# Delta-rule attention into a SwiGLU block on one core: products, sums and bank clears put in another order

## The chip, the cores and the metric

The kernel runs on one core of a Trainium2 chip. Its engines work side by side, each through its own queue in order: TensorE (PE in the profile; PEld is its weight loads), VectorE (DVE), ScalarE (ACT), GpSimd (POOL) and SyncE (SP), which issues the DMAs. The metric is the time of one execution on the device in microseconds (us); less is better. Before the change three executions took 687.78 us in the median (686.82 to 689.39).

## What is computed

Everything is float32. A delta-rule attention over 4 batches, 8 heads, 768 steps and a head size of 48 gives 3072 tokens of 384 numbers, and these go through a SwiGLU block with a hidden size of 1536:

```python
for t in range(S):
    kt, vt, bt = (k_n[:, :, t], v[:, :, t], beta[:, :, t, None])
    y[:, :, t] = np.einsum('bhd,bhde->bhe', q[:, :, t], state)
    v_old = np.einsum('bhde,bhd->bhe', state, kt)
    state = state + bt[:, :, :, None] * np.einsum('bhd,bhe->bhde', kt, vt - v_old)
...
g = x @ w_gate
silu = g * (1.0 / (1.0 + np.exp(-g)))
val = x @ w_val
return (silu * val @ w_out).astype(np.float32)
```

## The kernel before

**Tiling.** The 768 steps are cut into 12 chunks of 64 steps. A chunk has 4 x 64 = 256 tokens, which the kernel treats as two blocks of 128. The order of instructions on every engine is written out by hand: the order of the Python calls is the order in each engine's queue, and an instruction waits in its queue for the results it needs.

**What runs in a chunk.** For chunk c the feed-forward block runs: gate and value products, the elementwise product h, and the output product. Between its parts the attention of chunk c + 1 is slipped in by `point(c + 1)`, one step at a time: a step of `advance` (four in all; the last one transposes the result on TensorE and ScalarE copies it to `x_ffn`, the input x of the next chunk's feed-forward block, L1152 and L1153), or a step of preparation (transposes of keys and queries on VectorE, L470, and their products on TensorE, L497; a join, L870 to L888). `fill(n)` adds steps of a triangular inverse, with transposes on VectorE (L551) and a long run of small operations on GpSimd (L580, L586). Some points have a step left for TensorE and some have none.

**Rounds.** From chunk 2 on the gate and value products use a fast matrix product that needs fewer multiplications. `gate_val_fast(c, r, fill)` is one such round and makes six of the 24 blocks of h. Chunk 2 has one round (r = 0), the chunks 3 to 11 have two (r = 0 and r = 1): 19 rounds in all. A round is a fixed sequence of 15 products, named by number here as in the code: `multiply(p, n, c, r)` is product n, accumulated into the PSUM bank p. It is four matmuls, which the profile lists as eight matmul instructions of L1280 with eight weight loads. The banks are p4 (later called p2), p3 (later p6), p0 and p1 (later p5). Between the products VectorE adds and subtracts in PSUM (`plus` is L1510, `minus` is L1507) and ScalarE copies banks to the temporaries t0 and t1. `finish_h` lets ScalarE take the silu of one half of a bank (L1316) and VectorE multiply it with the other half (L1317). In a round the order on TensorE is: 4, 13, 1, 3, 2, a point, then 7, 11, 9, 0, 5, a point, then 6, 10, 8, 14, a point; product 12 follows at the head of the next round or of the output.

The banks tie products to VectorE. Product 5 accumulates into p0, where product 11 has put its result, so it can't start before `minus(t1, t1, p0)` has read p0. Product 6 accumulates into p0 again and can't start before `minus(p5, t0, p0)` has read what product 5 left. Product 8 goes into p6, which is the bank p3 where product 0 ended: `finish_h(c, r, 5, p3)` must have read it, and `minus(p6, t0, p2)` must have filled it anew.

**Sums of x.** Products 4, 3, 9, 14, 7, 5, 10, 6 and 8 take sums of blocks of x as their moving operand. `sums_of_x(c)` makes ten of them on VectorE; the first four (for products 3, 9, 14 and 4) are a chain, each adding to the one before. `x_sums(c)` calls it once, at the first call at which the four steps of `advance` for that chunk have been issued. `begin(c)` starts a chunk with product 4, which needs the fourth sum of the chain, then product 13, which needs none.

**Output.** `output_fast(c, fill)` has seven products of 12 matmuls with 192 columns (L1557). Two of its banks, p[1, 0] and p[1, 1], are begun by ScalarE writing zeros (`clear`, L1549), since the products that go in only accumulate. For the chunks after 2 the order is: first product, product 3, 2, 4, 5, a point, 6, the addition of the left half of o[1], its store, `x_sums(c + 1)`, product 7. In chunk 2 it is: first product, 5, 4, a point, 2, 3, a point, 7, store, `x_sums(3)`, 6, store. `first_product` clears p[1, 0], issues the product, copies it out and clears p[1, 1].

## Time and profile before

| what | value |
|---|---|
| median of three executions | 687.78 us (686.82 to 689.39) |
| the profiled execution | 689.76 us |
| its span, first to last instruction | 688.1 us |
| mean granted TensorE clock | 0.992 |
| DVE busy | 473.3 us (69%) |
| ACT busy | 256.1 us (37%) |
| POOL busy | 201.7 us (29%) |
| matmuls of L1280 on x_t and w_gv | 760, 102.4 us busy |
| matmuls of L1557 on wo_sb and h_f | 480, 84.2 us busy |
| sums and differences of 128x512 in PSUM, L1507 (ffn from p_sb and ffn) | 36, median 692 ns |
| sums of x, 128x128 (x_t from x_t and x_ffn, L1510) | 30, median 293 ns |

The profile shows one execution. Its own time, 689.76 us, is 1.7 us above its span, and 2.0 us above the median of the three. Matmuls overlap, so an instruction of 275 ns starts every 112 ns: the time of a product is read from one product's start to the next one's (0.89 us), not from the sum of its instructions. In rows of the timeline the first two numbers are start and duration in microseconds, then engine, line and operation, the tiles written and read, and in brackets how long the engine had been idle before and what ended that.

| stretch, us | PE busy | DVE busy | ACT busy | POOL busy | PE clock |
|---|---|---|---|---|---|
| 0 to 170 | 155.21 | 119.87 | 94.03 | 40.59 | 0.98 |
| 170 to 224 (chunk 2) | 50.74 | 40.52 | 17.86 | 38.56 | 0.97 |
| 280 to 330 (chunk 4) | 48.04 | 35.29 | 18.45 | 29.11 | 1.00 |
| 330 to 384 (chunk 5) | 53.21 | 35.12 | 16.88 | 11.81 | 1.00 |
| 540 to 590 (chunk 9) | 50.00 | 27.68 | 15.41 | 0.00 | 1.00 |

### The profile page before, as it was taken

How to read it: one execution, taken by the hardware profiler on the slowest of the kernel's cores; microseconds unless marked ns; L12 is line 12 of the kernel's file. 1: busy time of each engine (PE TensorE's matmuls, PEld its weight loads, DVE VectorE, ACT ScalarE, POOL GpSimd, SP SyncE). 2: the span in 40 equal slices, each digit the busy share in tenths (PEclk: the TensorE clock that was granted, in tenths of full speed). 3: DMA queues.
4: the chain of work that ended last, by engine and by line, in shares of the span. 5: the costliest groups of instructions: out<-in, count | busy, mean ns of one | idle time of the engine just before them, and what ended most of it. 6: DMA issues, size and time to landing. Idle time of an engine off the chain costs nothing.

```text
span 688.1 us, 24813 instructions
## 1 busy us (share of the span) xinstructions
PE 653.7 (95%) x10850; PEld 603.7 (88%) x10850; DVE 473.3 (69%) x982; ACT 256.1 (37%) x546; POOL 201.7 (29%) x309
## 2 busy tenths in 40 slices
PE   7788999998999999999999999999999999999997
PEld 4566888756988899999999999999999999999997
DVE  7987778798569867757767747767657655645462
ACT  5785765214332332334332244332232333132130
POOL 7130031104883030881030881030882000000000
PEclk9998999999999999999999999999999999999999
DMA  9767824016226352276262176242187122132220
GB/s 135 169 176 190 243 94 137 1 35 136 45 45 164 73 136 64 49 156 143 54 134 74 45 153 138 60 110 80 26 171 152 48 88 78 40 100 71 76 71 23
DMA packets 147437, 68.55 MB, mean 100 GB/s; under 512 B 123457, under 2 KB 126561, under 8 KB 147329
## 3 DMA queue, kind: packets, MB, share of 16 engines
q1 hardware_dynamic: 144992, 66.48, 40.2%
q8 instruction: 85, 1.39, 0.8%
q10 hardware_dynamic: 2080, 0.39, 0.4%
q0 software_dynamic: 256, 0.10, 0.1%
q14 instruction: 24, 0.19, 0.1%
HBM read 59.08 MB, written 7.86 MB: 97 GB/s over the span
## 4 chain that ended last, share of the span: by engine, by line
PE 64%; DVE 3%; issue 0%; DVEq 0%
PE ffn L1280 36%; PE ffn L1557 17%; PE p_px L1073 1%; PE p_px L1054 1%; PE p_py L497 1%; PE p_py L1127 1%; PE p_py L1044 1%; DVE x_t L1510 1%; DVE ffn L1507 1%; PE p_px L902 1%; PE p_px L497 1%; PE p_py L1152 1%; PE p_py L884 1%; PE p_px L870 1%; DVE o_sb L1510 0%
## 5 line engine op out<-in xcount | busy, mean ns | idle before, releaser
L1280 PE MATMUL ffn<-x_t,w_gv 128*128 128x128 f32 x760 | 102.4, 278 | 6.6 <-DVE x_t L1507 6.6
L1280 PEld LDWEIGHTS ffn<-x_t,w_gv 128*128 128x128 f32 x760 | 93.1, 193 | 8.3 <-issue 5.8
L1557 PE MATMUL ffn<-wo_sb,h_f 128*128 128x192 f32 x480 | 84.2, 329 | 0.6 <-ACT ffn L1549 0.6
L811 POOL TENSOR_TENSOR n_b<-mb,half 128x32 f32<-128x32 f32 x5 | 27.6, 5520 | 191.3 <-DVE mb L551 191.3
L1280 PE MATMUL ffn<-x_ffn,w_gv 128*128 128x128 f32 x600 | 80.0, 277 | 0.0
L1557 PEld LDWEIGHTS ffn<-wo_sb,h_f 128*128 128x128 f32 x480 | 77.8, 190 | 1.6 <-ACT ffn L1549 0.9
L1316 ACT ACTIVATE sil<-ffn 128x256 f32<-128x256 f32 x95 | 34.5, 382 | 114.6 <-PE ffn L1280 106.6
L586 POOL TENSOR_TENSOR zb<-zb,h_f 128x31 f32<-128x31 f32 (+15 forms) x124 | 71.9, 580 | 9.7
L1280 PEld LDWEIGHTS ffn<-x_ffn,w_gv 128*128 128x128 f32 x600 | 73.8, 194 | 0.0
L580 POOL TENSOR_TENSOR h_f<-zb,mb 128x31 f32<-128x31 f32 (+15 forms) x124 | 69.4, 560 | 14.4 <-DVE mb L568 5.0
L1280 PE MATMUL ffn<-x_t,h_f 128*128 128x128 f32 x464 | 63.6, 280 | 3.9 <-DVE ffn L1507 3.9
L1317 DVE TENSOR_TENSOR h_f<-sil,ffn 128x256 f32<-128x256 f32 x95 | 37.6, 418 | 42.8 <-ACT sil L1316 42.8
L1280 PEld LDWEIGHTS ffn<-x_t,h_f 128*128 128x128 f32 x464 | 56.3, 192 | 5.9 <-DVE ffn L1507 4.9
L1440 PE MATMUL ffn<-x_ffn,w_gv 128*128 128x256 f32 x216 | 48.0, 381 | 0.0
L1440 PEld LDWEIGHTS ffn<-x_ffn,w_gv 128*128 128x128 f32 x216 | 40.7, 190 | 5.6
L1510 DVE TENSOR_TENSOR o_sb<-o_sb,ffn 128x192 f32<-128x192 f32 x49 | 17.1, 349 | 31.5 <-PE ffn L1557 31.0
L1510 DVE TENSOR_TENSOR ffn<-ffn,p_sb 128x512 f32<-128x512 f32 x36 | 24.8, 693 | 16.2 <-PE ffn L1280 15.1
L1557 PE MATMUL ffn<-last_k,h_f 128*128 128x192 f32 x200 | 35.8, 326 | 0.0
L1440 PE MATMUL ffn<-x_t,w_gv 128*128 128x256 f32 x144 | 35.7, 400 | 0.0
L1557 PEld LDWEIGHTS ffn<-last_k,h_f 128*128 128x128 f32 x200 | 32.8, 190 | 0.0
L1440 PEld LDWEIGHTS ffn<-x_t,w_gv 128*128 128x128 f32 x144 | 27.7, 199 | 4.0
L1280 PE MATMUL ffn<-x_ffn,h_f 128*128 128x128 f32 x224 | 30.0, 277 | 0.0
(343 smaller groups left out, 1165.2 us busy)
## 6 DMA issues: line engine op xcount, KB each, us to landing
h_f<-w_s SPq DMA_DIRECT2D x81, 256.0 KB, 2.7
more_w<-w_s SPq DMA_DIRECT2D x27, 256.0 KB, 2.9
vin<-in_v_dram SPq DMA_DIRECT2D x48, 96.0 KB, 3.5
out_dram<-o_sb SPq DMA_DIRECT2D x48, 96.0 KB, 2.2
kn<-in_k_dram SPq DMA_DIRECT2D x20, 192.0 KB, 4.7
w_s<-h_f SPq DMA_DIRECT2D x10, 256.0 KB, 3.2
zt<-in_moe_w_out_dram SPq DMA_DIRECT2D x6, 384.0 KB, 4.4
qpad<-in_q_dram SPq DMA_DIRECT2D x36, 64.0 KB, 3.2
```

The lines of the kernel that those rows point to most:

```text
L497: nc.tensor.matmul(p_v[par][half_of(b if of_q else b ^ par), bp, j], kt[c][half_of(par), bp, j, b], xt[half_of(par), bp, j, b],)
L580: engine.tensor_tensor(out=t_v, in0=zb[:, 0 : j + 1, j : j + 1].to_broadcast([128, j + 1, m]), in1=mb[:, j : j + 1, j + 1 : R].to_broadcas ...
L586: engine.tensor_tensor(out=zb[:, 0 : j + 1, j + 1 : R], in0=zb[:, 0 : j + 1, j + 1 : R], in1=t_v, op=ALU.add,)
L811: nc.gpsimd.tensor_tensor(out=n, in0=mb.rearrange("p j i -> p (j i)")[:, 0 : R * R : R + 1], in1=half, op=ALU.pow,)
L870: nc.tensor.matmul(p_j[dst, c, m], a[lo, c, 2 * m + e, 0:R], zt[lo, c, 2 * m + e, R:C],)
L884: nc.tensor.matmul(p_j[hi, e, c, m], z1[row, c, m], t2[row, c, m])
L1280: nc.tensor.matmul(p[:, u], w(u), moving, start=start and u == 0, stop=True, skip_group_check=True,)
L1316: nc.scalar.activation(silu_of, p[:, 0:2], ACTF.Silu)
L1317: nc.vector.tensor_tensor(out=h_of(c, PAIRS[r][e % 3], e // 3), in0=silu_of, in1=p[:, 2:4], op=ALU.mult)
L1440: nc.tensor.matmul(ps[name][:, i], w_sb[:, t, (f + i) * 128 : (f + i + 1) * 128], xts[c][:, t], start=(t == 0 and i == 0), stop=(t == KT - 1),
L1510: nc.vector.tensor_tensor(out=out, in0=a, in1=b, op=ALU.add)
L1557: nc.tensor.matmul(p[x, part], a(f - f % 2)[:, f % 2], b(f), start=not begun and f == 0, stop=f == FH - 1, skip_group_check=True,)
```

## The change

Four things are put in another order; no operation is added or taken away.

1. In every round product 5 is issued ahead of product 0, and `minus(p5, t0, p0)` ahead of `finish_h(c, r, 5, p3)`. `load_late()`, which issues a waiting DMA if there is one, stays between the two products.
2. The chain of four sums of x is a function of its own. In the output of the chunks after 2 it is issued right behind product 6, ahead of the addition that empties p[1, 0]; the other six sums stay where all ten were.
3. In the output of chunk 2 all ten sums for chunk 3 are issued ahead of the second point and of product 7, instead of behind them.
4. In chunk 2 p[1, 1] is cleared together with p[1, 0], ahead of the first product, instead of behind the copy of that product's result.

```diff
-    def sums_of_x(c):
+    def first_sums_of_x(c):
         x = sums_x
         plus(x[3], x_of(c, 0, 0), x_of(c, 0, 2))
         plus(x[9], x[3], x_of(c, 1, 0))
         plus(x[14], x[9], x_of(c, 1, 2))
         minus(x[4], x[14], x_of(c, 1, 1))
+
+    def sums_of_x(c):
+        x = sums_x
         plus(x[8], x_of(c, 0, 0), x_of(c, 1, 0))
...
-    summed = set()
+    begun, summed = set(), set()
+
+    def first_x_sums(c):
+        if c < NCH and c not in begun and steps("advance", c) >= 4:
+            begun.add(c)
+            first_sums_of_x(c)
 
     def x_sums(c):
-        if c < NCH and c not in summed and steps("advance", c) >= 4:
+        first_x_sums(c)
+        if c in begun and c not in summed:
             summed.add(c)
             sums_of_x(c)
...
         multiply(p2, 9, c, r)
         minus(t1, t1, p0)
+        multiply(p0, 5, c, r)
+        load_late()
         multiply(p3, 0, c, r)
-        load_late()
-        multiply(p0, 5, c, r)
+        minus(p5, t0, p0)
         finish_h(c, r, 5, p3)
-        minus(p5, t0, p0)
         minus(p6, t0, p2)
...
         def first_product():
             clear(0)
+            if c == FAST:
+                clear(1)
             product(0, 0, lambda f: h_of(c, f, 0), quarter(0, 0))
             nc.scalar.copy(o[0][:, right], p[0, 0])
             more_sums_of_h(c)
             if c > FAST:
                 end_of_rounds()
-            clear(1)
+                clear(1)
...
             product_6()
+            first_x_sums(c + 1)
             plus(o[1][:, left], o[0][:, right], p[1, 0])
             store(c, 1, o[1])
             x_sums(c + 1)
...
             plus(o[1][:, right], o[1][:, right], p[1, 0])
+            x_sums(c + 1)
             point(c + 1)
             product_7()
             store(c, 0, o[0])
-            x_sums(c + 1)
             product_6()
```

## The prediction

> **What bounds the kernel now.** I read the page's busy times first, then who waited for whom on PE, then the chain that ended last, then the timeline at the places that these name.

> ```profile
> PE 653.7 (95%) x10850; PEld 603.7 (88%) x10850; DVE 473.3 (69%) x982; ACT 256.1 (37%) x546; POOL 201.7 (29%) x309
> ```
> ```profile
> PE ffn L1280 <- DVE ffn L1507: 7.9, 10, 0.8
> PE ffn L1280 <- DVE x_t L1507: 6.6, 5, 1.8
> ```

> PE is busy for 95% of the span: only its gaps can be won without removing work. From chunk 2 on, two waits (columns: us in total, times, longest) hold nearly all of them: ten in front of a product of L1280 for a subtraction in PSUM, and five for the last of the chained sums of x. The first kind in a round of chunk 4:

> ```profile
> 311.47 1.06 PE L1280 MATMUL ffn<-x_ffn,w_gv 128*128 128x128 f32 x8
> ...
> 312.36 1.06 PE L1280 MATMUL ffn<-x_t,h_f 128*128 128x128 f32 x8
> ...
> 312.56 0.69 DVE L1507 TENSOR_TENSOR p_sb<-p_sb,ffn 128x512 f32<-128x512 f32 x1 [1.31 <-PE ffn L1280]
> ...
> 313.14 0.97 PEld L1280 LDWEIGHTS ffn<-x_ffn,w_gv 128*128 128x128 f32 x8
> 313.25 1.06 PE L1280 MATMUL ffn<-x_ffn,w_gv 128*128 128x128 f32 x8
> ...
> 314.15 1.06 PE L1280 MATMUL ffn<-x_t,w_gv 128*128 128x128 f32 x8
> 314.35 0.38 ACT L1316 ACTIVATE sil<-ffn 128x256 f32<-128x256 f32 x1 [1.68 <-PE ffn L1280]
> ...
> 314.76 0.42 DVE L1317 TENSOR_TENSOR h_f<-sil,ffn 128x256 f32<-128x256 f32 x1 [1.51 <-ACT sil L1316]
> 315.24 1.29 DVE L1507 TENSOR_TENSOR ffn<-p_sb,ffn 128x512 f32<-128x512 f32 x2
> 315.99 0.97 PEld L1280 LDWEIGHTS ffn<-x_t,more_w 128*128 128x128 f32 x8 [0.98 <-DVE ffn L1507]
> 315.99 1.16 PE L1280 MATMUL ffn<-x_t,more_w 128*128 128x128 f32 x8 [0.79 <-DVE ffn L1507]
> ```

> The PE rows are products 11, 9, 0, 5 and 6. A product starts 0.89 us after the one before; its first weight load runs 0.11 ahead of it (313.14 to 313.25). Product 5 ends at 315.20, the subtraction into p5 starts at 315.24 and takes 0.69 (two share the row), and the load of product 6 comes 0.05 after its end. The load was due at 314.15 + 0.89 - 0.11 = 314.93 and came at 315.99: 1.06 us lost. Ten of the 19 rounds show this; in the other nine an attention step of PE lies between products 5 and 6.

> The second kind, at the end of chunk 3, and the clear in chunk 2:

> ```profile
> 281.63 2.11 PE L1557 MATMUL ffn<-wo_sb,h_f 128*128 128x192 f32 x12
> 281.83 0.35 DVE L1510 TENSOR_TENSOR o_sb<-o_sb,ffn 128x192 f32<-128x192 f32 x1 [1.38 <-PE ffn L1557]
> 282.10 0.72 DVE L1510 TENSOR_TENSOR x_t<-x_ffn 128x128 f32<-128x128 f32 x1
> ...
> 284.15 0.62 DVE L1507 TENSOR_TENSOR x_t<-x_t,x_ffn 128x128 f32<-128x128 f32 x1
> ...
> 284.88 0.97 PEld L1280 LDWEIGHTS ffn<-x_t,w_gv 128*128 128x128 f32 x8 [1.43 <-issue]
> ```
> ```profile
> 216.06 0.33 ACT L1549 COPY ffn<-mask_q 128x192 f32<-128x192 f32 x1
> ...
> 216.44 3.87 PEld L1557 LDWEIGHTS ffn<-wo_sb,h_f 128*128 128x128 f32 x24 [0.93 <-ACT ffn L1549]
> ```

> Product 7 of the output starts at 281.63, twelve matmuls at 0.1625 apart; the load of product 4 was due at 283.47 and came at 284.88, 0.11 after the fourth sum: 1.41 lost.

> **Part 1, products 5 and 0 exchanged.** Removed: 10 x 1.06 = 10.6 us, since product 0 (0.89) now lies between 5 and 6. Left of it: product 5's end to the load of product 6 still takes 0.04 + 0.69 + 0.05 = 0.78, while the load is due 0.89 - 0.11 - 0.16 = 0.62 after that end (a product ends 0.16 after the next one's start, 312.52 against 312.36). So 0.16 stays, ten times: 1.6 us.

> Added: product 5 must now follow `minus(t1, t1, p0)` behind product 9 alone. Before, 9 and 0 covered it. In the rows above the subtraction ends at 313.25, the load could come at 313.30 and is due at 313.14: 0.16 late. VectorE starts it 0.04 after product 11 in 16 of 19 rounds. In three (chunks 3, 5 and 7, r = 1) a copy of the join stands in front: it runs from 359.92 to 361.14, the subtraction to 361.86, the load comes at 361.91 instead of 361.44, 0.47 late. That makes 16 x 0.16 + 3 x 0.47 = 3.9 us. No row has a subtraction covered by just one product; from below the price is 0 (the load doesn't wait; a wait that is added can't gain), from above 1.06 per round (as where nothing covers it). I take the worked value: the same operation on the same bank type ends the ten waits.

> Queued behind the waits: product 0 waits with product 5, so the silu of `finish_h` starts 0.16 later than before and, on VectorE, behind the subtraction into p5. Does product 8 wait for it? In the round shown: load of 5 at 313.30, product 0 at 314.30, its end 315.36, silu 315.40 to 315.78, multiplication 315.81 to 316.23, subtraction into p6 to 316.85 at most. Product 6 comes at 315.25, 10 at 316.25, and the load of 8 is due at 317.03. That is 0.13 to spare; if it were gone, 0.1 to 0.3 in ten rounds. The VectorE work behind it ends 0.3 later while PE is 0.74 earlier. Where two transposes of L470 (2.4 us) follow, ScalarE's last silus and copies are that late too, and the clear of p[1, 0] behind them (323.61 to 323.92) moves to 324.03, for a load that was due at 324.62 and is now due at 323.88: 0.2 lost in chunks 4, 6 and 8, 0.6 us. `load_late` passes no reload (products 0 and 5 issue none), so SP's order stays.

> Part 1: 10.6 - 1.6 - 3.9 - 0.6 = 4.5 us gained.

> [...] The row at 315.99 shows the load waiting with its matmul, so I go by the row.

> **Part 2, chain of sums first.** Waits of this kind that the change can reach stand ahead of chunks 4, 6 and 8 (1.41 each) and of chunk 3; the fifth, ahead of chunk 2, is not touched. For chunks 5, 7, 9, 10 and 11 the sums are in time already (0.29 each, not 0.63). Behind the change the chain can start when x_ffn is copied (280.67 in chunk 3) and takes the 2.67 it took (282.10 to 284.77): done at 283.34, load 283.45, due 283.47. Gain 3 x 1.41 = 4.2 us at most, 0 at least: no sum comes later than it did. The addition behind the chain ends at 283.7 instead of 282.2; the copy that needs its bank comes after product 4 (ends 284.7). The store waits as long, and the reload queued behind it on SP is for a form used some ten products later.

> **Parts 3 and 4, chunk 2.** The load of output product 5 was due at 215.43 and came at 216.44; the second clear now runs behind the first, ended by 215.6, load at 215.65: 0.8 gained. Product 4 of chunk 3 was due at 228.90 and came at 230.30: 1.4. But the transposes of L470 now come behind ten sums, some 2.8 us later: keys are ready at 230.4 (229.7 with the 0.7 that chunk 2's round gains), and their product is due at 229.2. So 0.5 is given back: 1.7 together, from 0.3 to 2.2.

> **Sum.** 4.5 + 4.2 + 1.7 = 10.4 us. Against the profiled execution: span 688.1 to 677.7, time 689.76 to 679.4. The profiled execution lies 2.0 above the median; off the median it is 687.8 - 10.4 = 677.4.

> **Rivals.** (a) Only matmuls wait and loads run ahead of the wait: 29 waits are 0.11 shorter, 3.1 us, so 674.3. For it: at 284.88 the load came 0.03 ahead of its matmul (284.91). Against: in all ten waits for a PSUM bank the load came with the matmul. [...] (b) VectorE is late everywhere as in the three join rounds: 29 waits at 0.47 cost 13.6, part 1 becomes 10.6 - 13.6 - 0.6 = -3.6, and the whole gains 2.3: 685.5. For it: PE's gaps were VectorE's time to catch up, and the margins (0.13 at product 8, 0.02 at product 4) are thin. Against: in 16 rounds VectorE had been waiting for PE. (c) The chain isn't early, since `first_x_sums` does nothing unless the fourth step has been issued: 4.2 lost, 681.6. Against: the transposes of that step (L1152) stand ahead of product 6 in all these chunks. (d) Slower: product 5 becomes the wait of every round, VectorE still working off transposes and sums of h when product 11 ends. Each 0.1 us of lateness costs 2.9 us over the 29 waits, so it decides from 0.36 on; at 0.7 (half a transpose of L551, 1.2) it is 20.3 - 10.4 = 9.9 worse, 697.7. Against: in the busiest stretch with such rounds, 280 to 330, DVE is busy for 35.3 of 50 us.

> **How the numbers follow.** Forecast 0.58 (674.5 to 680.5 by itself), (a) 0.12, (b) 0.12, (c) 0.10, (d) 0.08. What a measurement can tell from no change is about 0.5%, 3.4 us: below 684.3 is faster, above 691.2 slower. Faster: forecast, (a), (c), 0.80; same: (b), 0.12; slower: (d), 0.08. The range leaves out (b) and (d), 0.20: from 673 (rival (a) and the 1 us by which runs differ) to 684.5.

> **What would show it.** No wait of 0.8 before product 6, but 19 short ones before product 5, product 9 to product 5 at 0.94 instead of 0.89, and 1.00 from there to product 0. The wait for x_t gone ahead of chunks 3, 4, 6 and 8. Wrong would be: a wait above 0.3 before product 5 or any before product 8; sums of x still behind the addition; the granted clock below 0.99.

## The result, and the profile after

The changed kernel takes 681.86 us in the median of five executions (679.86 to 684.13); the kernel before, run beside it, 687.78 (686.82 to 691.36). The ratio is 0.989, 95% interval 0.985 to 0.993: faster by 5.9 us, where 10.4 were forecast. The interval is a gain of 4.7 to 10.0 us, so the forecast gain lies just outside it.

The profiled executions have spans of 688.1 and 680.2 us, 7.9 apart. 2.06 of that lies ahead of 160 us, where the change touches nothing: the kernel before ran for 6.8 us at half TensorE clock there, from 62.9 on, the changed one for 3.4, from 37.5 on. From 160 us on the changed kernel is 5.84 ahead, and from here on only this is compared: the start of one and the same instruction in two traces, counted from an attention product (L1054) at about 160 us. The mean granted clock is 0.992 in both.

The busy times of the page after:

```profile
PE 657.2 (97%) x10850; PEld 606.2 (89%) x10850; DVE 474.5 (70%) x982; ACT 255.7 (38%) x546; POOL 197.1 (29%) x309
```

PE's share rose from 95 to 97%, but its busy time rose too, by 3.5 us, for the same instructions: what was won can't be read from this view.

The waits of weight loads after (us in total, times, longest):

```profile
PEld ffn L1290 <- DVE ffn L1520: 2.0, 1, 2.0
...
PEld ffn L1290 <- DVE ffn L1517: 1.6, 10, 0.2
...
PEld ffn L1290 <- DVE p_sb L1517: 1.2, 3, 0.4
```

Lines have moved by ten: L1290 is `multiply`, L1517 `minus`, L1520 `plus`. The ten waits of 0.8 have become ten of 0.16, as forecast; the three of 0.4 are the join rounds. The first line is new, and nothing forecast it. Of PE's five waits for sums of x, 6.6 us in all, one is left, ahead of chunk 2, which the change doesn't touch:

```profile
PE ffn L1290 <- DVE x_t L1517: 1.8, 1, 1.8
```

The round of chunk 4 that was shown of before, in the timeline of after:

```profile
309.95 1.06 PE L1290 MATMUL ffn<-x_t,h_f 128*128 128x128 f32 x8
...
310.90 1.16 PE L1290 MATMUL ffn<-x_t,w_gv 128*128 128x128 f32 x8
...
311.89 1.06 PE L1290 MATMUL ffn<-x_ffn,w_gv 128*128 128x128 f32 x8
...
312.16 0.70 DVE L1517 TENSOR_TENSOR ffn<-p_sb,ffn 128x512 f32<-128x512 f32 x1 [1.32 <-PE ffn L1290]
...
312.91 0.97 PEld L1290 LDWEIGHTS ffn<-x_t,more_w 128*128 128x128 f32 x8 [0.16 <-DVE ffn L1517]
312.92 1.16 PE L1290 MATMUL ffn<-x_t,more_w 128*128 128x128 f32 x8
```

These are products 9, 5, 0 and 6: 0.95 from 9 to 5 (forecast 0.94), 0.99 from 5 to 0 (1.00), and product 0 covers all but 0.16 of the subtraction into p5. The end of chunk 3, PE alone: product 4 of chunk 4 comes 1.95 after the output's product 7, twelve matmuls at 0.1625, without a wait.

```profile
280.48 2.11 PE L1567 MATMUL ffn<-wo_sb,h_f 128*128 128x192 f32 x12
282.43 1.05 PE L1290 MATMUL ffn<-x_t,w_gv 128*128 128x128 f32 x8
```

And the place that lost: products 2, 7, 11, 9 and 5 of chunk 3's round 0, PE alone, then the windows of the same time (PE, PEld, DVE, ACT and POOL busy, then the granted clock):

```profile
232.19 1.06 PE L1290 MATMUL ffn<-x_ffn,w_gv 128*128 128x128 f32 x8
235.06 1.77 PE L1290 MATMUL ffn<-x_t,h_f 128*128 128x128 f32 x8 [1.81 <-DVE ffn L1520]
236.63 1.91 PE L1290 MATMUL ffn<-x_ffn,w_gv 128*128 128x128 f32 x8
238.34 1.30 PE L1290 MATMUL ffn<-x_t,more_w 128*128 128x128 f32 x8
239.47 1.06 PE L1290 MATMUL ffn<-x_t,w_gv 128*128 128x128 f32 x8
```
```profile
235.00:236.00 1.00, 0.94 (x6) 0.94 (x7) 0.61 (x2) 0.63 (x2) 0.00 (x0) 0.71 0.87 158
236.00:237.00 1.00, 1.00 (x6) 1.00 (x6) 0.00 (x0) 0.13 (x1) 0.00 (x0) 0.50 0.98 109
```

PE waits 1.81 us for `plus(p1, p0, t0)`, and the three products behind it take 1.57, 1.71 and 1.13 instead of 0.89 to 0.95: the granted clock is 0.71 and 0.50 in the windows shown, and 0.50 in the next. The kernel before had neither the gap nor the half clock here (products 7, 11, 9 and 0 at 237.48, 238.48, 239.37 and 240.26).

Term by term, from 160 us on (minus is a gain):

| term | forecast, us | measured, us |
|---|---|---|
| ten stalled rounds | -7.4 (-0.74 each) | -6.7 (-0.63 in chunk 2, -0.67 in the others) |
| six rounds without a stall | +1.0 (+0.16 each) | +0.9 (+0.15 each) |
| three join rounds | +1.4 (+0.47 each) | +1.4 (+0.46 each) |
| clear of p[1, 0] in chunks 4, 6 and 8 | +0.6 (0.2 each) | +0.3 (0.14 in 4 and 6, none seen in 8) |
| sums ahead of chunks 4, 6 and 8 | -4.2 (-1.41 each) | -4.2 (-1.40 or -1.41 each) |
| parts 3 and 4 | -1.7 | +1.75 |
| PE idle at L870 in chunk 5, with `issue` alone named (last section) | none | +0.76 |
| sum | -10.4 | -5.8 |

Of the ten stalled rounds one, chunk 3's round 0, lies inside the stretch of parts 3 and 4. It is taken at -0.67, and the 1.75 is what is left. That stretch runs from the last L902 product ahead of chunk 2's output (211.79 in the trace before) to the first join product L870 of chunk 3 (246.77): 34.97 us before, 36.05 after, and 36.05 - 34.97 + 0.67 = 1.75.

### The profile page after: what moved, and what is told of

Read it like the earlier page. It is cut to its first block, busy times and chain, and to the rows that moved or that the text cites. A ratio compares the mean times of both kernels' runs of the same rounds, so it can differ in the third digit from the quotient of the medians.

```text
span 680.2 us, 24832 instructions
## 1 busy us (share of the span) xinstructions
PE 657.2 (97%) x10850; PEld 606.2 (89%) x10850; DVE 474.5 (70%) x982; ACT 255.7 (38%) x546; POOL 197.1 (29%) x309
## 3 DMA queue, kind: packets, MB, share of 16 engines
q8 instruction: 85, 1.39, 0.8%
## 4 chain that ended last, share of the span: by engine, by line
PE 90%; DVE 6%; ACT 2%; issue 2%; DVEq 0%
PE ffn L1290 38%; PE ffn L1567 20%; PE ffn L1450 11%; PE ffn L1477 4%; PE p_px L1054 2%; PE p_px L1073 2%; PE p_py L1044 1%; PE p_px L902 1%; PE p_py L497 1%; PE p_py L1127 1%; PE p_px L497 1%; PE p_py L1152 1%; PE p_px L631 1%; PE p_px L870 1%; PE p_py L884 1%
## 5 line engine op out<-in xcount | busy, mean ns | idle before, releaser
L1290 PE MATMUL ffn<-x_t,w_gv 128*128 128x128 f32 x760 | 103.5, 280 | 2.4 <-DVE x_t L1517 1.8
L1290 PEld LDWEIGHTS ffn<-x_t,w_gv 128*128 128x128 f32 x760 | 93.1, 192 | 4.7 <-DVE x_t L1517 2.0
L1290 PE MATMUL ffn<-x_ffn,w_gv 128*128 128x128 f32 x600 | 81.0, 279 | 0.0
L580 POOL TENSOR_TENSOR h_f<-zb,mb 128x31 f32<-128x31 f32 (+15 forms) x124 | 71.0, 572 | 14.4 <-DVE mb L568 5.0
L1290 PEld LDWEIGHTS ffn<-x_ffn,w_gv 128*128 128x128 f32 x600 | 74.7, 196 | 0.0
L586 POOL TENSOR_TENSOR zb<-zb,h_f 128x31 f32<-128x31 f32 (+15 forms) x124 | 69.5, 561 | 9.7
L1290 PE MATMUL ffn<-x_t,h_f 128*128 128x128 f32 x464 | 64.2, 282 | 1.8 <-DVE ffn L1520 1.8
L1290 PEld LDWEIGHTS ffn<-x_t,h_f 128*128 128x128 f32 x464 | 56.9, 193 | 3.7 <-DVE ffn L1520 2.0
L1517 DVE TENSOR_TENSOR ffn<-p_sb,ffn 128x512 f32<-128x512 f32 x36 | 25.1, 696 | 24.4 <-PE ffn L1290 23.8
L1520 DVE TENSOR_TENSOR ffn<-ffn,p_sb 128x512 f32<-128x512 f32 x36 | 24.7, 692 | 19.4 <-PE ffn L1290 16.2
L1450 PE MATMUL ffn<-x_t,w_gv 128*128 128x256 f32 x144 | 33.9, 385 | 0.0
L1520 DVE TENSOR_TENSOR o_sb<-o_sb,ffn 128x192 f32<-128x192 f32 x49 | 16.9, 347 | 20.6 <-PE ffn L1567 20.2
L1290 PE MATMUL ffn<-x_ffn,h_f 128*128 128x128 f32 x224 | 30.3, 279 | 0.0
```

What stands on the lines that cost most here:

```text
L580: engine.tensor_tensor(out=t_v, in0=zb[:, 0 : j + 1, j : j + 1].to_broadcast([128, j + 1, m]), in1=mb[:, j : j + 1, j + 1 : R].to_broadcas ...
L586: engine.tensor_tensor(out=zb[:, 0 : j + 1, j + 1 : R], in0=zb[:, 0 : j + 1, j + 1 : R], in1=t_v, op=ALU.add,)
L1290: nc.tensor.matmul(p[:, u], w(u), moving, start=start and u == 0, stop=True, skip_group_check=True,)
L1450: nc.tensor.matmul(ps[name][:, i], w_sb[:, t, (f + i) * 128 : (f + i + 1) * 128], xts[c][:, t], start=(t == 0 and i == 0), stop=(t == KT - 1),
L1517: nc.vector.tensor_tensor(out=out, in0=a, in1=b, op=ALU.subtract)
L1520: nc.vector.tensor_tensor(out=out, in0=a, in1=b, op=ALU.add)
```

## The experiments

Two theories of chunk 3's start stood against each other. T1: VectorE has no idle time left between chunk 2's rounds and `plus(p1, p0, t0)`, so whatever PE gains on the way comes back as a wait at product 7, and one long wait is followed by half clock. T2: the parts add up as forecast, and what is missing is chance. For T1 speak the windows of VectorE in the trace before (busy time, instructions, clock, DMA share, GB/s):

```profile
205.00:210.00 5.00, 4.90 (x8) 1.00 0.64 81
...
215.00:220.00 5.00, 4.93 (x8) 1.00 0.58 159
...
225.00:230.00 5.00, 4.90 (x10) 1.00 0.00 0
230.00:235.00 5.00, 4.82 (x14) 1.00 0.34 82
```

From 200 to 235 us VectorE is busy for 34.29 of 35 us, and from 199.3 until that addition ends it has no pause above 0.1 us. In the trace before `plus(p1, p0, t0)` ended at 237.43 and product 7 started at 237.48 (its row, from the timeline of VectorE):

```profile
236.74 0.69 DVE L1510 TENSOR_TENSOR ffn<-ffn,p_sb 128x512 f32<-128x512 f32 x1
```

VectorE was already what product 7 came behind, with no gap on PE to show it. After, that addition ends 0.36 us earlier by the common count, and so does product 7, although PE had been 2.25 ahead one product earlier (product 2: 236.50 and 232.19, less the 2.06 of the start).

All eleven kernels of this section, with both kernels of the change, in one table. "Stretch" is L902 to L870 as above; "from 160 us" is the whole trace behind that point against before; the ratio is of times to before, which was run again beside each group of kernels (medians 687.78 to 689.94), so the ratios can be compared and the medians only roughly. Each kernel was profiled once. Gaps are PE's idle time ahead of product 4 of chunk 3, and ahead of product 7 (11 where it comes first).

| kernel | gap at 4 | gap at 7 | half clock behind it | stretch | from 160 us | median us, ratio (95%) |
|---|---|---|---|---|---|---|
| before | 1.23 | 0 | no | 34.97 | 0 | |
| after | 0 | 1.81 | yes | 36.05 | -5.84 | 681.86, 0.989 (0.985 to 0.993) |
| no_part3 | 1.57 | 0.26 | no | 34.67 | -6.95 | 683.15, 0.990 (0.987 to 0.993) |
| no_part4 | 0 | 1.82 | yes | 36.06 | -4.23 | 681.50, 0.990 (0.986 to 0.994) |
| two_cover | 0 | 1.81 | yes | 36.27 | -8.18 | 678.12, 0.984 (0.981 to 0.987) |
| two_cover_no3 | 1.57 | 0.21 | no | 34.62 | -7.87 | 680.88, 0.988 (0.985 to 0.991) |
| split_sums | 0 | 1.21 | no | 33.87 | -6.45 | 683.30, 0.991 (0.987 to 0.994) |
| w_later | 0 | 0.95 | no | 32.79 | -7.83 | 680.56, 0.988 (0.984 to 0.992) |
| w_later_no3 | 1.12 | 0.27 | no | 33.58 | -8.12 | 681.89, 0.991 (0.987 to 0.994) |
| w_later_two | 0 | 1.59 | no | 33.40 | -11.50 | 678.35, 0.984 (0.980 to 0.989) |
| all_three | 0 | 0.16 | no | 31.83 | -11.76 | 676.08, 0.979 (0.975 to 0.983) |
| part1_only | 1.57 | 0.27 | no | 34.65 | -1.77 | 686.19, 0.995 (0.992 to 0.997) |
| part2_only | 1.47 | 0.26 | no | 35.22 | -3.44 | 685.08, 0.994 (0.992 to 0.997) |

**One part alone.** `part1_only` keeps the exchange of products 5 and 0 and undoes the rest; `part2_only` keeps the early chain of sums and undoes the rest.

> Part 1 alone, in the kernel before. Theory 1: each of the ten rounds with the old wait gains 0.67, each of the other nine loses 0.15 or (three join rounds) 0.46, 0.4 is lost at the clears of three chunks, and the gain of chunk 2's round is swallowed by VectorE's full queue at the start of chunk 3: about 3.5 us, 684.3. Theory 2 (the sum of the prediction): 4.5 us, 683.3. In the trace both expect ten starts of product 6 0.05 to 0.1 late instead of 0.95, and product 5 late in all 19 rounds.

> Part 2 alone (the chain of four sums first, in the chunks after 2), in the kernel before. Theory 1: product 4 of chunks 4, 6 and 8 comes 1.40 earlier each, nothing is given back: 4.2 us, 683.6. Rival: VectorE then does the other six sums and the addition later against PE, and the products of keys (L497) wait for their transposes: 3 us or less, 684.8 or more.

With part 1 alone the rounds gain 4.0 us, as in the changed kernel. The trace gains only 1.8. It lost time in three places where `issue` alone is named (see the last section): 1.06 and 0.58 between L870 and L884 in two chunks, and 0.27 at L1044. And the 0.34 by which PE was ahead at the end of chunk 2 is gone at product 7 of chunk 3, where PE waits for VectorE (1.57 ahead of product 4 and 0.27 ahead of product 7, before 1.23 and 0): that T1 had expected. With part 2 alone the starts of chunks 4, 6 and 8 come earlier by 1.40 or 1.41 each, to the hundredth what the prediction worked out, and 0.8 is lost elsewhere, mostly in three steps of 0.2 to 0.3, one of them at the start of chunk 3, which that edit doesn't touch. Both parts are real and independent; both alone are faster by their times, by 0.5 and 0.6%. These ratios are 3.6 and 4.1 us, near T1's 3.5 and 4.2, though the medians themselves (686.19 and 685.08, beside 689.94 for before) lie above the expected ones.

**Part 3 undone.**

```diff
             plus(o[1][:, right], o[1][:, right], p[1, 0])
-            x_sums(c + 1)
             point(c + 1)
             product_7()
             store(c, 0, o[0])
+            x_sums(c + 1)
```

> The changed kernel with part 3 undone: in chunk 2 the ten sums for chunk 3 stand behind product 7 and its store again. Theory 1: from the output of chunk 2 to product 7 of chunk 3's first round VectorE's queue is full, so PE can't get further ahead there; part 3 only gathers the waits into one gap of 1.8 us, and behind it TensorE ran at half clock for 3.4 us (1.7 us lost). Then this kernel is faster than the changed one by 1.5 to 2.5 us (about 680 us), the half clock at the start of chunk 3 is gone, and the time from the transposes L1152 of chunk 2's output to the join product L870 in chunk 3 is below 26.4 us (28.1 with the change, 26.3 before). Theory 2: the half clock fell into that one execution by chance and part 3 is worth the 0.9 us of the prediction: this kernel is slower than the changed one by about 0.9 us (682.7), and the stretch takes the same or more.

In the timeline of this kernel, PE alone, products 4, 7 and 11 of chunk 3:

```profile
225.13 1.13 PE L1290 MATMUL ffn<-x_t,w_gv 128*128 128x128 f32 x8 [1.57 <-DVE x_t L1517]
...
232.31 1.16 PE L1290 MATMUL ffn<-x_t,h_f 128*128 128x128 f32 x8 [0.26 <-DVE ffn L1520]
233.31 1.06 PE L1290 MATMUL ffn<-x_ffn,w_gv 128*128 128x128 f32 x8
```

The wait for the sums is back, and 1.57 + 0.26 is 1.83: the sum of the waits is that of the changed kernel, 1.81. Part 3 takes no waiting time away; it gathers it in one place. Only there does half clock follow, and the stretch is 1.38 us longer with part 3 than without. T1's numbers were missed: from L1152 to L870 it takes 26.76 us, not less than 26.4, and the time is 683.15, not about 680. The times can't tell this kernel from the changed one (683.15 and 681.86, ranges overlapping).

**Part 4 undone**: `clear(1)` again behind the copy of the first product's result, in every chunk.

> The changed kernel with part 4 undone: p[1, 1] is cleared behind the copy again, so product 5 of chunk 2's output comes 0.74 us later. Theory 1: VectorE sets when product 7 of chunk 3 can start, so the 0.74 comes out of the gap ahead of it: at product 7 and behind it nothing is lost, the gap is 1.0 instead of 1.8 us, and with the shorter gap the half clock may stay away. Rival (parts add up): the whole is 0.74 us slower than the changed kernel.

T1 had expected a shorter gap at product 7, since PE comes later by 0.74 us; the gap is 1.82. What T1 had overlooked is that VectorE stops PE once more on the way: with part 4 the output's products in p[1, 0] wait 0.4 for an addition of VectorE (`o_sb`, L1520), without part 4 there is no such wait, and at L497 of chunk 3 the two kernels are only 0.07 apart (18.92 and 18.99 behind L902). The stretch is 36.05 and 36.06: in this company part 4 is worth nothing.

**VectorE relieved.** In `w_later` three sums of weights (1.9 us on VectorE) leave chunk 2's output for the end of chunk 3's round 0; `w_later_no3` is the same without part 3.

```diff
         finish_h(c, r, 3, p2)
         if r > 0:
             sums_of_h(c, 8)
+        if (c, r) == (FAST + 1, 0):
+            sums_of_w(1, (3, 9, 10))
...
             differences()
-            sums_of_w(1, (3, 9, 10))
```

> The changed kernel, but three sums of weights that VectorE makes in chunk 2's output (0.6 to 0.7 us each, 1.9 together) are made at the end of chunk 3's first round, where they are needed next. Theory 1 (VectorE's queue is full up to product 7 of chunk 3, the amount of work sets the time): product 7 comes 1.8 us earlier, the gap ahead of it is gone or below 0.3, TensorE doesn't fall to half clock there (1.7 more), so the stretch from the transposes L1152 of chunk 2's output to the join product L870 in chunk 3 shrinks from 28.1 to about 24.7 us; the whole is 3 us or more better than the changed kernel. Rival (only the order of ten sums ahead of the transposes L470 matters, or the half clock was chance): the gap stays above 1.2 us or the stretch above 26.

> The same with part 3 undone: it tells what part 3 is worth once VectorE has room. Theory 1: now the sums for chunk 3 are late for product 4 again while VectorE waits for nobody, so this kernel is slower than the one with part 3 by 0.5 to 1.4 us in the stretch from L1152 to L870 (25.2 to 26.1). Rival (part 3 does harm by itself): it is as fast or faster.

The half clock is gone and the stretch is 3.26 us shorter (from L1152 it is 24.87, 24.7 expected), but the gap fell only to 0.95, not below 0.3, and the time is 1.3 us better than that of the changed kernel, not 3 or more. The gap: `plus(p1, p0, t0)` came 1.78 earlier in the trace, as expected, while PE, no longer stopped for the output's addition, came earlier too. With the room so made part 3 is worth 33.58 - 32.79 = 0.8 us; without it, it cost 1.4. That change of sign is T1's, and T2 has nothing for it, though each of the four stretches comes from one profile. (The whole of `w_later_no3` from 160 us on holds 1.6 us that are not the edit's: there was no half clock at chunk 2's start, where seven matmuls of product 4 took 1.05 us and the changed kernel's eight 1.70.)

**A later place for three sums of x.** In `split_sums` the sums for products 10, 5 and 6 of chunk 3 come where VectorE had been idle for 2.97 us.

```diff
         minus(x_less(c), x_of(c, 0, 0), x_of(c, 0, 1))
         minus(x[7], x_of(c, 0, 1), x[8])
+        if c != FAST + 1:
+            last_sums_of_x(c)
+
+    def last_sums_of_x(c):
+        x = sums_x
         plus(x[10], x[7], x_of(c, 1, 1))
...
         plus(p2, p3, t1)
+        if (c, r) == (FAST + 1, 0):
+            last_sums_of_x(c)
```

> The changed kernel, but in front of chunk 3 only the chain and the sums for products 8 and 7 stay ahead of the second point; the last three sums (products 10, 5 and 6) come behind plus(p2, p3, t1) of chunk 3's round 0, where VectorE is idle for 2.97 us. Nothing is left out. T1 (VectorE's unbroken run of work sets product 7 of that round, and the gap's length sets the half clock): the run is 0.74 shorter (225.99 to 226.73), so the gap ahead of product 7 is about 1.07 instead of 1.81, no half clock behind it, and the stretch from L1152 in chunk 2 to L870 in chunk 3 is 28.14 - 0.74 - 1.7 = 25.7 us. T2 (the half clock at that place is chance, or hangs on something else than the gap): the gap shrinks, the half clock stays, 27.4. T3 (the stall goes elsewhere: product 9 or 5 waits for the late sums): 28.1 with a new wait for x_t.

Products 7 and 11 of chunk 3 in its timeline, PE alone:

```profile
236.58 1.16 PE L1295 MATMUL ffn<-x_t,h_f 128*128 128x128 f32 x8 [1.21 <-DVE ffn L1527]
237.58 1.06 PE L1295 MATMUL ffn<-x_ffn,w_gv 128*128 128x128 f32 x8
```

The gap is 1.21 (T1: 1.07), the products behind it come at 1.00 and 0.89, no half clock, and the stretch from L1152 to L870 is 25.95 (T1: 25.7; T2: 27.4; T3: 28.1). The late sums delay nothing. The median time, 683.3 us, is no better than that of the changed kernel: the profiled execution lost 2.1 us behind this stretch in three steps (0.65, 0.50 and 0.91); from 160 us on its list of PE's waits has four with `issue` alone named, 1.4 us in all.

**Two products over each subtraction.** `two_cover` issues product 11 ahead of 7, so that 7 and not only 9 stands between 11 and 5; `two_cover_no3` undoes part 3 on top, `w_later_two` moves the three sums of weights, and `all_three` moves the three sums of x as well.

```diff
-        multiply(p1, 7, c, r)
         multiply(p0, 11, c, r)
+        multiply(p1, 7, c, r)
         nc.scalar.copy(t0, p1)
-        multiply(p2, 9, c, r)
         minus(t1, t1, p0)
+        multiply(p2, 9, c, r)
         multiply(p0, 5, c, r)
```

> The changed kernel with product 11 ahead of product 7, so that two products (7 and 9) and not one (9) lie between product 11 and product 5. Theory 1: the 0.155 lost ahead of product 5 in 16 rounds is gone, the 0.46 in the three rounds behind a join copy stays: 2.5 us better than the changed kernel, 679.4; product 9 to product 5 is 0.89 again. Rival: the product isn't late for lack of cover but for its place behind another wait: no difference, 681.9.

> The changed kernel with product 11 ahead of product 7 and with part 3 undone (the ten sums for chunk 3 behind product 7 of the output again). Nothing is left out. T1: the same 1.8 of stall as with part 3, but split (about 1.57 ahead of product 4, the rest ahead of product 11), no half clock; some 1.1 to 1.7 better in the trace than the same kernel with part 3, so -9.3 or better against before from 160 us on. T2: half clock in about as many profiles as with part 3, no steady difference, -8.2.

> All that helps together: the changed kernel, product 11 ahead of product 7 in every round, the three sums of weights later. Theory 1: 2.5 us from the first (as measured in the trace of that kernel alone) and 3 from the second: 5.5 us better than the changed kernel, about 676 on the scale on which it takes 681.9. Rival: one of the two is taken back by the other, 678 or more.

> Three edits together on the changed kernel: product 11 ahead of product 7, the sums of weights for chunk 3 moved to the end of its round 0, and the last three sums of x for chunk 3 behind plus(p2, p3, t1). Nothing is left out. T1: VectorE's run is 1.8 + 0.74 shorter, the gap ahead of product 11 about 0.85 (1.59 - 0.74) or less, no half clock; 0.7 better than the version with the first two edits alone, 677 to 677.7 us. T2: half clock at chunk 3 as likely as before, 679. T3: a new wait for x_t takes the 0.7 back.

The 0.15 of the rounds is gone (0.00 in the six, -0.82 instead of -0.67 in the stalled ones); the 0.46 of the join rounds stays. In the trace that is 2.3 us, 2.5 expected. Chunk 3's start keeps its 1.81 and its half clock in `two_cover`, and loses the half clock without part 3 (the three products behind the gap at 7 take 1.17, 1.71 and 1.53 us with it and 0.99, 0.89 and 0.90 without): stretches of 36.27 and 34.62, the 1.4 of the first pair once more (1.65). Over the whole trace that pair stands at -8.18 and -7.87 only, since the second lost 0.82, 0.47 and 0.36 elsewhere; T1 had expected -9.3 or better for it and missed, and by times the one with part 3 is ahead (678.12 and 680.88).

`w_later_two` has a gap of 1.59 where `w_later` had 0.95: its chunk 2 started without half clock (a granted clock of 1.00 from 171 to 176 us), so that PE was 1.8 us further than in `w_later` at L902, and product 11, behind VectorE's addition, came only 1.0 earlier than product 7 there. Its time, 678.35, is the rival's number and not the 676 expected; in the trace it is 5.7 better than the changed kernel (5.5 expected), but the missing half clock at chunk 2, which isn't the edit's, is about 1.8 of that. In `all_three`, products 11 and 7 of chunk 3, PE alone:

```profile
238.72 1.16 PE L1295 MATMUL ffn<-x_ffn,w_gv 128*128 128x128 f32 x8 [0.16 <-DVE ffn L1529]
239.71 1.06 PE L1295 MATMUL ffn<-x_t,h_f 128*128 128x128 f32 x8
```

The gap is 0.16, less than the 0.85 that T1 gave as its upper end, and the stretch 31.83. With 676.08 us this is the fastest version; its ratio to before, 0.975 to 0.983, lies wholly below that of the change, 0.985 to 0.993. (The execution that was profiled is the slowest of its four, 682.19: its mean granted clock is 0.979, that of the other three 0.989 to 0.995.)

T1 stands as far as the traces go: the gap at product 7 follows what VectorE has to do before it, and half clock followed it in the three profiles with 1.81 or 1.82 at product 7 and in none of the other nine edits. T2 falls for this stretch. The 1.4 that part 3 costs there is the half clock's: without the 1.6 us of it the stretch would be about as long with part 3 as without (34.45 and 34.67). What stays open is how often the half clock falls there in executions that were not profiled; the times do not separate the kernels with and without part 3.

## Why the forecast came out as it did

The direction and the two large terms were right, and the time lies inside the range; the gain was 10.4 forecast and 5.9 measured. That the trace gives almost the same (5.84 from 160 us on) is in part luck, since 0.76 of it was lost to a wait in chunk 5 that comes in some profiles and not in others.

**Part 1** held as a mechanism. Product 0 covers the subtraction, product 5 waits a little in every round, and join rounds cost 0.46 against 0.47. The ten stalled rounds gained 0.67 instead of 0.74. The step "0.16 stays, ten times" was mis-sized by 0.07: a product that starts behind a wait takes 1.16 instead of 1.06 (310.90 against 311.89), so the subtraction into p5 starts 1.26 us behind product 5's start (312.16) where the rows of before had 1.09. Ten times 0.07 is 0.7 us. Product 8 never waited, so the margin of 0.13 held; the clears cost 0.14 where 0.2 was taken. (16 x 0.16 + 3 x 0.47 is 4.0, not 3.9; that changes nothing here.)

**Part 2** was exact: three times 1.41 was forecast, 1.40 or 1.41 was measured. The load that was forecast at 0.02 ahead of its due time came in time.

**Parts 3 and 4** hold the step that failed: "keys are ready at 230.4 (229.7 with the 0.7 that chunk 2's round gains), and their product is due at 229.2. So 0.5 is given back: 1.7 together". The working followed the keys and no further. At their products, where it had 0.5 given back, PE lost nothing: by the common count it was 2.08 ahead at product 4, in front of them, and 2.25 at product 2, behind them. But behind the two transposes of L470 VectorE still had L551, L841, L846 and L536 to do, some 5 us, and only then `plus(p1, p0, t0)`, which product 7 waits for. In the timeline of VectorE after, the last row holding that addition and the next:

```profile
229.52 1.21 DVE L551 STREAM_TRANSPOSE zt<-zb 128x512 f32<-128x512 f32 x1
...
233.11 1.29 DVE L536 TENSOR_TENSOR p_sb<-p_py,mask_q 128x512 f32<-128x512 f32 x2
234.32 1.29 DVE L1520 TENSOR_TENSOR ffn<-ffn,p_sb 128x512 f32<-128x512 f32 x2
```

In the trace before that addition ended just as product 7 was due. Part 3 gave PE 1.4 us, part 4 and chunk 2's round 1.4 more, and VectorE 0.36 in all, so PE's lead was handed back at the output's addition and at product 7. Then three products ran at half clock, for 1.6 us more. The lower end of the term, 0.3 gained, left out a loss altogether, and it came out at 1.75 lost: a miss of 3.45 us, most of the missing 4.6. With the 0.7 of the rounds and the 0.76 of idle time in chunk 5, less 0.3 from the clears, that is all of it. The 0.76 is a wait that the forecast had put at nothing: the last section has the trace at that place.

The prediction's table had VectorE at 40.52 of 54 us for 170 to 224. That mean hides the 35 us in which it hardly paused. The same view in steps of 5 us would have shown it.

**The rivals.** (a) fell: at 312.91 and 312.92 the load and its matmul wait together, and the ten waits of loads are 0.16. No load passed a wait of its matmul for a bank: in all ten it starts 0.001 or 0.002 us ahead of it, against the 0.11 without a wait. (b) fell: 0.46 only in the three join rounds. (c) fell: the chain is early in all three chunks. (d) fell in the rounds, where no load of product 5 waited longer than 0.4. Its idea, VectorE as the bound, was right in one place that it did not name.

Of the signs that were to show a wrong forecast, "a wait above 0.3 before product 5" was badly set: the three join rounds wait 0.4, and the forecast itself had 0.47 there. The mean granted clock was no use: 0.992 before and after, since 3.4 us of half clock had gone from the first 100 us while 3.4 came at chunk 3.

## What to carry to other kernels

Before a wait is taken from one engine, look at the other engine in windows as short as the stretch concerned: if it has no idle time up to the next place where the first one waits for it, the wait is only moved, as 1.57 and 0.26 us were into 1.81 here. Work that is put ahead in a queue must be followed to every consumer behind it, not only to the first. And two short waits can be cheaper than one long wait of the same sum: here the stretch with 1.57 and 0.26 was 1.38 us shorter than the one with 1.81, behind which the granted clock was 0.50.

## What the runs showed of the hardware

That the idle time in such a step is what counts is the author's estimate from these five; a limit was not shown. Of the gaps in the table, 1.81 or 1.82 us ahead of product 7 was followed by half clock in all three profiles that had it, and 0.95 to 1.59 as the longest gap in none of nine. At chunk 2's start the length of the gap alone does not separate them: behind 1.84 us the changed kernel's second product took 1.70 instead of 0.89, and behind 1.59 that of `all_three` took 1.71, while behind 1.84 `w_later_two` had a granted clock of 1.00, and behind 1.58 `w_later_no3` took the 1.05 us for seven matmuls named above.

**PE idle with `issue` alone named.** In the nine profiles whose waits from 160 us on were listed, PE stood still for 0.2 to 0.9 us at none to four places with only "issue" named as the cause, so with no event in the profile to wait for. In chunk 5 of the changed kernel it is this place:

```profile
348.82 0.38 PE L870 MATMUL p_px<-zt,a_sb 32*32 32x32 f32 x20 [0.55 <-issue]
```

The DMA packets of the same trace show what came ahead of it. The page has a queue for instructions (packets, MB, share):

```profile
q8 instruction: 85, 1.39, 0.8%
```

These 85 packets have 16 KB each, and the trace has 21857 instructions of PE (matmuls, weight loads and 157 others), 257 for a packet. The seven idle times of the changed kernel's trace that have only "issue" named end whole numbers of times 256 such instructions apart, each 1.39 to 1.72 us after a packet of this queue had landed. So a packet is taken to hold 256, an estimate from these counts. By it, none of the 74 packets behind the first ten was begun sooner than 1.23 us after it had landed (before: 1.29). The packet for chunk 5's L870 landed at 347.42; PE had finished all before it at 348.28 and went on at 348.82. In the kernel before it landed at 349.90, and its first matmul started at 351.71 without a gap. That PE waited for the packet is the author's reading of these times. L870 is a likely place by it, since its 128 loads and 128 matmuls of 32x32, as many instructions as that estimate gives a packet, take 1.29 us.

A wait of this kind at L870 stands in five of the lists of the seven profiles with part 1, 0.5 to 0.9 us long, and in neither of the two without it (`before` and `part2_only`). One profile per kernel can't tell whether part 1 makes it likelier, and why the packet came late stays open. Together with the half clock of the first 100 us (6.8 us of it before, 3.4 after) it fits that executions of one kernel lie 2 to 11 us apart, and that effects of 1 to 2 us show in the traces and not in the times.
